# Chunk-selecting attention with a soft mixture of experts: selection masks of two score groups side by side in 32-row strips, and a new order of pair and slot steps

## The chip, the cores and the metric

The kernel runs on one core of a Trainium2 chip. The metric is the device time of one execution in microseconds (us); lower is better. A core has a matrix engine (PE, which writes only to the accumulator memory PSUM), a vector engine (DVE), an activation engine (ACT), a general engine (POOL, which here masks tiles and issues most DMAs) and a DMA-issuing engine (SP). Each engine works through its own list of instructions in order; semaphores tie the lists together.

## The reference

`q`, `k`, `v` have shape (4 batches, 8 heads, 768 positions, 64). For every query an upper bound of its score with each of 24 chunks of 32 keys decides which 6 chunks it may look at; then comes ordinary causal attention over these chunks. The result, seen as a 3072 x 512 matrix, goes through a soft mixture of 8 experts with 4 slots each.

```python
k_min = np.min(k_chunks, axis=3); k_max = np.max(k_chunks, axis=3)
ub = np.sum(np.maximum(q * k_min, q * k_max), axis=-1)        # per query and chunk
ub = np.where(causal, ub, -1e9)
top_chunks = np.argsort(ub, axis=-1)[..., -6:]
scores = scale * (q @ k.T), where (key's chunk in top_chunks) and (key <= query), else -1e9
attn = softmax(scores) @ v
x = attn as (3072, 512)
logits = x @ phi                                               # 32 slots
slot_input = softmax(logits over all 3072 rows).T @ x
slot_out = per expert: relu(slot_input @ w1) @ w2
out = softmax(logits over slots) @ slot_out
```

## The kernel before

Work goes by pairs of heads: 16 pairs, 4 to a batch, the two heads of a pair in the upper and lower 64 partitions. `qT` and `kT` hold a pair's queries and keys transposed (64 + 64 partitions x 768).

**Pair steps.** `transposes` and `evac_T` make `kT` and `qT` (PE into the PSUM tile `tr_ps`, then one ACT copy each). `kmin`, `kmax`, `qsplit` (DVE) and `ubound` (PE) give the chunk bounds in `ub_ps`; `ubound` starts each of its six query tiles with a matmul of its own that adds the causal bound (L229), followed by two matmuls (L234). `select` (twelve MAX8 and one compare on DVE, one small cast on POOL) writes to `ns_t`, for each query, a 1 at every chunk that is not selected, and the row's largest bound. `ns_transposes` and `evac_ns` turn it round into `nsT`, so that a matmul with the fixed matrix `smask` can add a large negative number to the scores of chunks that are left out.

**Scores.** The causal half of a pair's score matrix is cut into six groups, `GROUPS` 0 to 5, of widths 512, 512, 512, 512 (in two pieces of 256), 512 (384 and 128) and 128 per head. `scores(i, g)` issues for each piece a K.Q matmul for each head (L274) and then a mask matmul for each head (L280). Both kinds work on 64 rows, the two heads on different rows. A group's PSUM tile `sc_ps` has one bank for each head. `expo(i, g)` is one ACT exponential over the whole group (L292), followed by POOL's causal select of the diagonal blocks (L294). `pv` multiplies with V (L311), `normalise` divides (L324), `x_transposes` and `evac_x` store the pair's output transposed.

**Slot steps**, once per batch: `moe_logits`, `moe_copy`, `moe_max`, `moe_bound` (the maximum of the logits over rows), `moe_exp` (broadcast by PE, subtraction on DVE, exponential on ACT, rescaling of the running sum `si_acc`), `moe_comb` (exponentials over slots into `c_pad`), `moe_dispatch` (slot inputs, 30 matmuls into `si_ps`) and `moe_ct` (transposes of `c_pad`).

**Buffers.** PSUM is full: `p_sc` has two `sc_ps` tiles, `p_at` one tile for `pv`, and `p_tp` two buffers that all other PSUM tiles (`ub_ps`, `tr_ps` of keys and of queries, `xT_ps`, `ns_ps`, `pmT_ps`, `bc_ps`, `si_ps`, `cT_ps`, `lg_ps`) take in turn in the order of issue. So the first write to such a tile waits until the tile two before it in this order has been read out.

**Order.** It is written out by hand in one loop, and no scheduler changes it (`tc.manual_schedule()`). Iteration `i` handles the scores of pair `i`, the bounds of pair `i + 1`, the transposes of pair `i + 2`, `pv` of pair `i - 1` and the normalisation of pair `i - 2`; slot steps of a batch are put in at `i - 2` and `i - 3` past its last pair. In outline:

```python
scores/expo 0, scores/expo 1, [moe_max], ubound, normalise, [moe_bound], select,
transposes k + ACT copy, loads, pv 0-2, [moe_exp], scores/expo 2, scores/expo 3,
x_transposes, pv 3, transposes q + ACT copy, kmin, evac_x, kmax, [moe_comb], loads,
scores/expo 4, scores/expo 5, ns_transposes + evac_ns, pv 4, [moe_dispatch], pv 5,
qsplit, [moe_ct], [moe_logits, moe_copy]
```

After the loop come the last pairs' normalisation, the last batch's slot steps, the experts and the output.

Of the kernel before, what the change touches and what calls it, by code (L numbers as in the profile page):

```python
# [10 lines left out]
F32 = mybir.dt.float32  # L11
BF16 = mybir.dt.bfloat16
ALU = mybir.AluOpType
ACT = mybir.ActivationFunctionType
# [4 lines left out]
CH = 32  # L19
NCHUNK = 24  # L20
NQT = 6
P = 128
# [24 lines left out]
def kernel(  # L47
# [10 lines left out]
    nc = tc.nc  # L58
# [18 lines left out]
    st = {}  # L77
# [23 lines left out]
    smask = static.tile([P, NQT, 4, CH], BF16, name="smask")  # L101
    schunk = static.tile([P, NCHUNK, 1], BF16, name="schunk")
    headsel = static.tile([P, 1, 2, 1], BF16, name="headsel")
    ns_t = [static.tile([P, NQT, 2, 64], BF16, name=f"ns_t{i}") for i in range(2)]

    small = ctx.enter_context(tc.tile_pool(name="small", bufs=1))
    xp = ctx.enter_context(tc.tile_pool(name="xp", bufs=2))
# [50 lines left out]
        out=caus[:4], in_=caus[:4], compare_op=ALU.is_ge, fill=NEG, base=0,  # L158
        pattern=[[4, NQT], [0, 2], [-1, NCHUNK]], channel_multiplier=1,
    )  # L160
    for h in range(2):
        sl = schunk[h * 64:(h + 1) * 64]
        nc.gpsimd.affine_select(
            out=sl, in_=sl, compare_op=ALU.not_equal, fill=NEG, base=0,
            pattern=[[-1, NCHUNK], [0, 1]], channel_multiplier=1,
        )
        nc.gpsimd.affine_select(
            out=sl, in_=sl, compare_op=ALU.not_equal, fill=-1.0, base=-NCHUNK,
            pattern=[[0, NCHUNK], [0, 1]], channel_multiplier=1,
        )  # L170
# [54 lines left out]
    def ubound(i):  # L225
        ps = p_tp.tile([P, NQT, 2 * NCHUNK], F32, name="ub_ps", tag="tp")
        qpn, bd = st.pop(("qpn", i)), st.pop(("bd", i))
        for t in range(NQT):
            nc.tensor.matmul(  # L229
                ps[:, t, :], lhsT=qgrp.rearrange("p a b -> p (a b)"),  # L230
                rhs=caus[:, t].rearrange("p h c -> p (h c)"), start=True, stop=False,
            )
            for x in range(2):
                nc.tensor.matmul(  # L234
                    ps[:, t, :], lhsT=qpn[:, x, t * P:(t + 1) * P],
                    rhs=bd[:, x].rearrange("p h c -> p (h c)"),
                    start=False, stop=(x == 1),
                )
        st["ubps", i] = ps

# [12 lines left out]
    def ns_transposes(i):  # L253
        ps = p_tp.tile([P, NQT, P], BF16, name="ns_ps", tag="tp")
        for t in range(NQT):
            nc.tensor.matmul(  # L256
                ps[:, t, :], lhsT=ns_t[i % 2][:, t].rearrange("p h c -> p (h c)"),
                rhs=ident, is_transpose=True,
            )
        st["nsps", i] = ps  # L260

    def evac_ns(i):
# [1 line left out]
        nc.vector.tensor_copy(t, st.pop(("nsps", i)).rearrange("p t c -> p (t c)"))  # L264
        st["nsT", i] = t

    def scores(i, g):
        ps = p_sc.tile([P, 2, 512], F32, name="sc_ps", tag="sc")
        kT, qT, nsT = st["kT", i], st["qT", i], st["nsT", i]
        for kg, q0, w, c in GROUPS[g]:  # L270
            qs = slice(kg * P + q0, kg * P + q0 + w)
            for h in range(2):
                r = slice(h * 64, (h + 1) * 64)
                nc.tensor.matmul(  # L274
                    ps[:, h, c:c + w], lhsT=kT[r, kg * P:(kg + 1) * P], rhs=qT[r, qs],
                    start=True, stop=False,
                )
            for h in range(2):
                r = slice(h * 64, (h + 1) * 64)
                nc.tensor.matmul(  # L280
                    ps[:, h, c:c + w], lhsT=smask[r, kg].rearrange("p a b -> p (a b)"),
                    rhs=nsT[r, qs], start=False, stop=True,
                )
        st["scps", i, g] = ps

    def expo(i, g):
        w = WIDTH[g]
        if g < 5:
            e = ep.tile([P, 2, 512], BF16, name="e_sb", tag="e_sb")
        else:  # L290
            e = ep5.tile([P, 2, P], BF16, name="e5_sb", tag="e5_sb")
        nc.scalar.activation(e[:, :, :w], st.pop(("scps", i, g))[:, :, :w], func=ACT.Exp, scale=scale)  # L292

        nc.gpsimd.affine_select(  # L294
            out=e[:, :, :P], in_=e[:, :, :P], compare_op=ALU.is_ge, fill=0.0,
            base=0, pattern=[[0, 2], [1, P]], channel_multiplier=-1,
        )
        st["e", i, g] = e
# [81 lines left out]
        nc.vector.tensor_reduce(mb, pmT, axis=AX.X, op=ALU.max)  # L380
        st["mb", b] = mb

    def moe_exp(b):
        lg = st["lg", b]
        bc = p_tp.tile([P, NS], F32, name="bc_ps", tag="tp")
        nc.tensor.matmul(
            bc, lhsT=st.pop(("mb", b)).broadcast_to([NS, P]), rhs=identf[:NS, :NS], start=True, stop=True,
        )
        m_new, m_old = m_run[b % 2], m_run[(b + 1) % 2]
        if b == 0:  # L390
            nc.vector.tensor_copy(m_new, bc)
        else:
            nc.vector.tensor_tensor(m_new, m_old, bc, op=ALU.max)
        ld = small.tile([P, NQT, NS], F32, name="ld", tag="ld")
        nc.vector.tensor_tensor(
            ld, lg, m_new.rearrange("p (o s) -> p o s", o=1).broadcast_to([P, NQT, NS]), op=ALU.subtract,
        )
        d_sb = small.tile([P, NQT, NS], BF16, name="d_sb", tag="d_sb")
        nc.scalar.activation(d_sb, ld, func=ACT.Exp)
        st["d", b] = d_sb  # L400
        if b > 0:

            dm = small.tile([P, 1, NS], F32, name="dm", tag="dm")
            nc.vector.tensor_tensor(dm[:, 0, :], m_old, m_new, op=ALU.subtract)
            nc.scalar.activation(dm, dm, func=ACT.Exp)
            if b == B - 1:
                moe_comb(b)
            nc.vector.tensor_tensor(si_acc, si_acc, dm.broadcast_to([P, NDG + 1, NS]), op=ALU.mult)

    def moe_comb(b):  # L410

        lg = st.pop(("lg", b))
        rm = small.tile([P, NQT, 1], F32, name="rm", tag="rm")
        nc.vector.tensor_reduce(rm, lg, axis=AX.X, op=ALU.max)
        lc = small.tile([P, NQT, NS], F32, name="lc", tag="lc")
        nc.vector.tensor_tensor(lc, lg, rm.broadcast_to([P, NQT, NS]), op=ALU.subtract)

        for g in range(2):
            nc.scalar.activation(
                c_pad[:, :, :, g * SPE:(g + 1) * SPE],  # L420
                lc[:, :, g * 16:(g + 1) * 16].rearrange("p t (j s) -> p t j s", j=4), func=ACT.Exp,
            )
# [27 lines left out]
    def have(i):  # L450
        return 0 <= i < NPAIR

    def moe(step, i):

        if have(i) and i % NPB == NPB - 1:
            step(i // NPB)
# [15 lines left out]
    for i in range(-2, NPAIR):  # L472
        if i >= EARLY:
            wt = ctx.enter_context(tc.tile_pool(name=f"wt{i}", bufs=1))
            w_sb.append(wt.tile([P, NFG * Dm], BF16, name=f"w_sb{i}"))
            weights(i)
        if have(i):
            scores(i, 0)
            expo(i, 0)
            scores(i, 1)  # L480
            expo(i, 1)
        moe(moe_max, i - 3)
        if have(i + 1):
            ubound(i + 1)
        if have(i - 2):
            normalise(i - 2)
        moe(moe_bound, i - 3)
        if have(i + 1):
            select(i + 1)
        if have(i + 2):  # L490
            transposes(i + 2, "k")
            evac_T(i + 2, "k")
        if have(i + 4) and i >= -1:
            load(i + 4, "k")
            load(i + 4, "q")
        if have(i - 1):
            pv(i - 1, [0, 1, 2])
        moe(moe_exp, i - 3)
        if have(i):
            scores(i, 2)  # L500
            expo(i, 2)
            scores(i, 3)
            expo(i, 3)
        if have(i - 2):
            x_transposes(i - 2)
        if have(i - 1):
            pv(i - 1, [3])
        if have(i + 2):
            transposes(i + 2, "q")
            evac_T(i + 2, "q")  # L510
            kmin(i + 2)
        if have(i - 2):
            evac_x(i - 2)
        if have(i + 2):
            kmax(i + 2)
        moe(moe_comb, i - 3)
        if have(i + 2) and i >= 0:
            load_v(i + 2)
        if i < EARLY:
            weights(i)  # L520
        if have(i):
            scores(i, 4)
            expo(i, 4)
            scores(i, 5)
            expo(i, 5)
        if have(i + 1):
            ns_transposes(i + 1)
            evac_ns(i + 1)
        if have(i - 1):
            pv(i - 1, [4])  # L530
        moe(moe_dispatch, i - 3)
        if have(i - 1):
            pv(i - 1, [5])
        if have(i + 2):
            qsplit(i + 2)
        moe(moe_ct, i - 3)
        moe(moe_logits, i - 2)
        moe(moe_copy, i - 2)
        if i == LAST - 2:
            l_ctx.close()  # L540
        if i == LAST - 1:
            u_ctx.close()
# [21 lines left out]
    moe_copy(B - 1)  # L564
    moe_max(B - 1)
    moe_bound(B - 1)
    moe_exp(B - 1)
    moe_dispatch(B - 1)


# [88 lines left out]
    n = 0  # L659
# [46 lines left out]
```

## Time and profile before

| | us |
|---|---|
| median of 3 runs | 177.5 (176.98 to 177.66) |
| the profiled execution | 178.38 |
| its span in the trace | 176.7 |
| PE busy in the span | 139.9 (79%) |
| DVE busy | 127.9 (72%) |
| ACT busy | 119.8 (68%) |
| POOL busy | 99.8 (57%) |

The profiled execution took 1.7 us more than the span that the trace shows, and 0.9 us more than the median. Three views are used. The page sums up each engine and the costliest groups of instructions. The windows view gives each engine's busy time within a stretch. The timeline lists instructions in order of time: start, length, engine, line, what is written and read, how many of them were merged, and in brackets the idle time ahead with what ended it. Matmuls overlap, so that the distance from one start to the next, and not the length, tells how long PE is taken. The head loop runs from the first exponential at 16.94 us to about 137 us.

### The profile page before, as it was taken

Reading aid. Unit: us, or ns where it says so; the run is one execution under the profiler, and the core shown is the slowest. Engines: PE = TensorE matmul, PEld = TensorE weight load, DVE = VectorE, ACT = ScalarE, POOL = GpSimd, SP = SyncE. Lnnn points to the kernel's source line nnn. Section 1 sums busy time; section 2 is a strip of 40 time slices with the busy share of each in tenths; the row PEclk is TensorE's granted clock in tenths of the full one; section 3 lists DMA queues with packets and bytes.
Section 4 is the critical chain, followed back from the end, with each engine's and each line's share of the span. In section 5 each row is a group of like instructions: output and inputs, shape, how many; then the busy total and the mean of one; then the engine's idle time right before and its main releaser. Section 6 shows DMA issues by size and latency. Waiting matters only on the chain.

```text
span 176.7 us, 5992 instructions
## 1 busy us (share of the span) xinstructions
PE 139.9 (79%) x2485; PEld 96.1 (54%) x2486; DVE 127.9 (72%) x429; ACT 119.8 (68%) x163; POOL 99.8 (57%) x194
## 2 busy tenths in 40 slices
PE   0447989999989889999988999999689569976400
PEld 0333656667667667766766776676467443532000
DVE  4177759999999998999998999999752650247530
ACT  2414799889889868988977698898668321156430
POOL 8975677887779657878774676659344600000000
PEclk9999999999999999999999999999999956999855
DMA  3999999999999999999999999299999994009995
GB/s 41 152 183 165 208 209 200 205 201 201 183 214 189 210 183 123 208 174 206 164 139 201 170 198 149 22 182 210 194 213 218 211 217 81 4 6 403 401 406 211
DMA packets 40459, 32.92 MB, mean 186 GB/s; under 512 B 26352, under 2 KB 34544, under 8 KB 40432
## 3 DMA queue, kind: packets, MB, share of 16 engines
q0 software_dynamic: 38416, 26.25, 101.2%
q1 hardware_dynamic: 2016, 6.29, 9.0%
q8 instruction: 19, 0.31, 0.7%
q14 instruction: 8, 0.07, 0.1%
HBM read 52.49 MB, written 6.29 MB: 333 GB/s over the span
## 4 chain that ended last, share of the span: by engine, by line
PE 37%; ACT 22%; POOL 11%; DVE 11%; DMA 10%; issue 6%; POOLq 0%; DVEq 0%; ACTq 0%
ACT e_sb L292 17%; PE sc_ps L274 7%; DMA out_dram<-o_sb 5%; PE at_ps L311 5%; PE sc_ps L280 5%; DMA k_in<-in_k_dram 4%; POOL e_sb L294 4%; PE tr_ps L187 3%; PE h_ps L603 3%; DVE x_sb L324 3%; POOL q_in L132 2%; PE so_ps L638 2%; POOL k_in L132 2%; PE si_ps L430 2%; PE ns_ps L256 2%
## 5 line engine op out<-in xcount | busy, mean ns | idle before, releaser
L292 ACT ACTIVATE e_sb<-sc_ps 128x1024 bf16<-128x1024 f32 x96 | 83.6, 935 | 11.8 <-PE sc_ps L280 10.9
L294 POOL TENSOR_SCALAR_AFFINE_SELECT e_sb<-e_sb 128x256 bf16<-128x256 bf16 x96 | 39.4, 421 | 32.9 <-ACT e_sb L292 32.1
L274 PE MATMUL sc_ps<-qT,kT 64*128 64x512 bf16 (+3 forms) x256 | 40.3, 315 | 5.7 <-ACT e_sb L292 5.4
L280 PE MATMUL sc_ps<-nsT,smask 64*128 64x512 bf16 (+3 forms) x256 | 37.4, 311 | 0.5 <-DVE nsT L264 0.5
L311 PE MATMUL at_ps<-v_t,e_sb 128*128 128x65 bf16 x672 | 29.4, 194 | 1.2 <-DVE x_sb L324 1.1
L311 PEld LDWEIGHTS <-e_sb 128*128 128x128 bf16 x672 | 25.1, 98 | 3.4 <-DVE x_sb L324 1.6
L274 PEld LDWEIGHTS <-kT 64*128 64x128 bf16 x256 | 15.7, 95 | 16.0 <-issue 8.2
L245 DVE MAX8 mx<-ub_ps 128x8 f32<-128x24 f32 x192 | 18.8, 172 | 5.7 <-PE ub_ps L234 5.6
L205 DVE TENSOR_REDUCE mm<-kT 128x24 bf16<-128x768 bf16 x16 | 15.2, 950 | 5.8 <-ACT kT L196 5.8
L137 POOL DMA_DIRECT2D v_t<-in_v_dram x16 | 16.7, 1042 | 2.0 <-PE ns_ps L256 1.3
L196 ACT COPY kT<-tr_ps 128x768 bf16<-128x768 bf16 x16 | 12.8, 803 | 5.4 <-PE tr_ps L187 5.4
L280 PEld LDWEIGHTS <-smask 64*128 64x128 bf16 x256 | 13.3, 96 | 5.6 <-issue 1.5
L324 DVE TENSOR_TENSOR x_sb<-at_ps,inv 128x768 bf16<-128x768 f32 (+2 forms) x17 | 15.5, 911 | 0.6
L211 DVE TENSOR_REDUCE mm<-kT 128x24 bf16<-128x768 bf16 x16 | 15.1, 943 | 0.0
L187 PE MATMUL tr_ps<-ident,k_in 128*64 128x128 bf16 x192 | 9.4, 240 | 6.4 <-DMA k_in<-in_k_dram 5.3
L196 ACT COPY qT<-tr_ps 128x768 bf16<-128x768 bf16 x16 | 13.2, 825 | 0.9 <-PE tr_ps L187 0.9
L668 DVE TENSOR_SCALAR o_sb<-o_ps,cinv 128x512 f32<-128x512 f32 x12 | 8.6, 747 | 7.1 <-PE o_ps L666 4.5
L132 POOL DMA_DIRECT2D k_in<-in_k_dram x16 | 11.7, 728 | 0.9 <-issue 0.5
L234 PE MATMUL ub_ps<-bd,qpn 128*128 128x48 bf16 x192 | 10.2, 187 | 2.3 <-DVE qpn L221 2.2
L670 ACT ACTIVATE o_sb<-o_ps,cinv 128x512 f32<-128x512 f32 x12 | 7.8, 688 | 5.7 <-DMA out_dram<-o_sb 3.3
L229 PEld LDWEIGHTS <-qgrp 128*128 128x128 bf16 x96 | 8.0, 98 | 6.7 <-issue 6.7
L132 POOL DMA_DIRECT2D q_in<-in_q_dram x16 | 11.5, 716 | 0.0
(95 smaller groups left out, 213.3 us busy)
## 6 DMA issues: line engine op xcount, KB each, us to landing
w_sb<-in_moe_w_dram POOLq DMA_DIRECT2D x16, 1024.0 KB, 11.5
out_dram<-o_sb SPq DMA_DIRECT2D x10, 512.0 KB, 5.5
k_in<-in_k_dram POOLq DMA_DIRECT2D x16, 192.0 KB, 7.3
q_in<-in_q_dram POOLq DMA_DIRECT2D x16, 192.0 KB, 7.9
v_t<-in_v_dram POOLq DMA_DIRECT2D x16, 192.0 KB, 7.6
out_dram<-o_sb SPq DMA_DIRECT2D x4, 256.0 KB, 3.4
phi_sb<-in_moe_phi_dram POOLq DMA_DIRECT2D x1, 32.0 KB, 8.7
```

The lines of the kernel that those rows point to most:

```text
L132: nc.gpsimd.dma_start(out=t, in_=src.rearrange("h (p g) d -> p h (g d)", p=P))
L137: nc.gpsimd.dma_start(out=v_t[i % NV][:, :, :, :D], in_=v[b, 2 * j:2 * j + 2].rearrange("h (g p) d -> p h g d", p=P),)
L196: nc.scalar.copy(t.rearrange("d (p g) -> d p g", g=NQT), st.pop((nm + "ps", i)).rearrange("d g p -> d p g"),)
L205: nc.vector.tensor_reduce(mm[:, 0, 0, :], kT, axis=AX.X, op=ALU.min)
L211: nc.vector.tensor_reduce(mm[:, 1, 0, :], kT, axis=AX.X, op=ALU.max)
L245: nc.vector.max(mx[:, a, :], ub[:, a, :])
L274: nc.tensor.matmul(ps[:, h, c:c + w], lhsT=kT[r, kg * P:(kg + 1) * P], rhs=qT[r, qs], start=True, stop=False,)
L280: nc.tensor.matmul(ps[:, h, c:c + w], lhsT=smask[r, kg].rearrange("p a b -> p (a b)"), rhs=nsT[r, qs], start=False, stop=True,)
L292: nc.scalar.activation(e[:, :, :w], st.pop(("scps", i, g))[:, :, :w], func=ACT.Exp, scale=scale)
L294: nc.gpsimd.affine_select(out=e[:, :, :P], in_=e[:, :, :P], compare_op=ALU.is_ge, fill=0.0, base=0, pattern=[[0, 2], [1, P]], channel_mult ...
L311: nc.tensor.matmul(o, lhsT=st["e", i, g][:, h, c:c + P], rhs=v_t[i % NV][:, h, kg, :], start=(kg == 0), stop=(kg == t),)
L324: nc.vector.tensor_tensor(st["x", b][:, t0:t1, 2 * j:2 * j + 2, :].rearrange("p t h d -> p h t d"), at[:, :, :, :D], inv.broadcast_to([P, ...
```

## The change

- `ns_t` has 32 columns for each head in place of 64, and `ns_transposes` transposes it twice for each query tile, into partitions 0 to 63 and 64 to 127 (12 matmuls in place of 6): the mask operand then stands in four strips of 32 partitions, two copies of two heads. `schunk`, from which `smask` is made, is filled for four strips in place of two.
- `scores(i, g0)` handles two groups at once: the K.Q matmuls of both groups, each of 64 rows as before, and then the mask matmuls of both, each of 32 rows in a strip of its own. `expo` of the two groups follows.
- `ubound` adds the causal bound with one matmul of 288 columns in place of six of 48.
- `moe_exp` is split into `moe_shift` (PE and DVE), `moe_exp` (the two exponentials) and `moe_rescale`; `moe_comb` into `moe_comb` (DVE) and `moe_weights` (ACT).
- The order: `pv` 4 and `ns_transposes` with `evac_ns` stand ahead of groups 4 and 5; `moe_max` and `moe_bound` stand there too, behind them; `moe_shift` and `moe_comb` stand at the end of the iteration; `moe_exp`, `moe_rescale`, `moe_weights`, `moe_dispatch` and `moe_ct` come one iteration later than before.

```diff
@@ -101,7 +101,7 @@
     smask = static.tile([P, NQT, 4, CH], BF16, name="smask")
     schunk = static.tile([P, NCHUNK, 1], BF16, name="schunk")
     headsel = static.tile([P, 1, 2, 1], BF16, name="headsel")
-    ns_t = [static.tile([P, NQT, 2, 64], BF16, name=f"ns_t{i}") for i in range(2)]
+    ns_t = [static.tile([P, NQT, 2, CH], BF16, name=f"ns_t{i}") for i in range(2)]
 
     small = ctx.enter_context(tc.tile_pool(name="small", bufs=1))
     xp = ctx.enter_context(tc.tile_pool(name="xp", bufs=2))
@@ -158,8 +158,8 @@
         out=caus[:4], in_=caus[:4], compare_op=ALU.is_ge, fill=NEG, base=0,
         pattern=[[4, NQT], [0, 2], [-1, NCHUNK]], channel_multiplier=1,
     )
-    for h in range(2):
-        sl = schunk[h * 64:(h + 1) * 64]
+    for r in range(4):
+        sl = schunk[r * CH:(r + 1) * CH]
         nc.gpsimd.affine_select(
             out=sl, in_=sl, compare_op=ALU.not_equal, fill=NEG, base=0,
             pattern=[[-1, NCHUNK], [0, 1]], channel_multiplier=1,
@@ -225,16 +225,16 @@
     def ubound(i):
         ps = p_tp.tile([P, NQT, 2 * NCHUNK], F32, name="ub_ps", tag="tp")
         qpn, bd = st.pop(("qpn", i)), st.pop(("bd", i))
+        nc.tensor.matmul(
+            ps.rearrange("p t c -> p (t c)"), lhsT=qgrp.rearrange("p a b -> p (a b)"),
+            rhs=caus.rearrange("p t h c -> p (t h c)"), start=True, stop=False,
+        )
         for t in range(NQT):
-            nc.tensor.matmul(
-                ps[:, t, :], lhsT=qgrp.rearrange("p a b -> p (a b)"),
-                rhs=caus[:, t].rearrange("p h c -> p (h c)"), start=True, stop=False,
-            )
             for x in range(2):
                 nc.tensor.matmul(
                     ps[:, t, :], lhsT=qpn[:, x, t * P:(t + 1) * P],
                     rhs=bd[:, x].rearrange("p h c -> p (h c)"),
-                    start=False, stop=(x == 1),
+                    start=False, stop=(t == NQT - 1 and x == 1),
                 )
         st["ubps", i] = ps
 
@@ -253,10 +253,11 @@
     def ns_transposes(i):
         ps = p_tp.tile([P, NQT, P], BF16, name="ns_ps", tag="tp")
         for t in range(NQT):
-            nc.tensor.matmul(
-                ps[:, t, :], lhsT=ns_t[i % 2][:, t].rearrange("p h c -> p (h c)"),
-                rhs=ident, is_transpose=True,
-            )
+            for r in range(2):
+                nc.tensor.matmul(
+                    ps[r * 64:(r + 1) * 64, t, :], lhsT=ns_t[i % 2][:, t].rearrange("p h c -> p (h c)"),
+                    rhs=ident, is_transpose=True,
+                )
         st["nsps", i] = ps
 
     def evac_ns(i):
@@ -264,24 +265,32 @@
         nc.vector.tensor_copy(t, st.pop(("nsps", i)).rearrange("p t c -> p (t c)"))
         st["nsT", i] = t
 
-    def scores(i, g):
-        ps = p_sc.tile([P, 2, 512], F32, name="sc_ps", tag="sc")
+    def scores(i, g0):
         kT, qT, nsT = st["kT", i], st["qT", i], st["nsT", i]
-        for kg, q0, w, c in GROUPS[g]:
-            qs = slice(kg * P + q0, kg * P + q0 + w)
-            for h in range(2):
-                r = slice(h * 64, (h + 1) * 64)
-                nc.tensor.matmul(
-                    ps[:, h, c:c + w], lhsT=kT[r, kg * P:(kg + 1) * P], rhs=qT[r, qs],
-                    start=True, stop=False,
-                )
-            for h in range(2):
-                r = slice(h * 64, (h + 1) * 64)
-                nc.tensor.matmul(
-                    ps[:, h, c:c + w], lhsT=smask[r, kg].rearrange("p a b -> p (a b)"),
-                    rhs=nsT[r, qs], start=False, stop=True,
-                )
-        st["scps", i, g] = ps
+        tiles = [p_sc.tile([P, 2, 512], F32, name="sc_ps", tag="sc") for _ in range(2)]
+        for n, ps in enumerate(tiles):
+            for m, (kg, q0, w, c) in enumerate(GROUPS[g0 + n]):
+                qs = slice(kg * P + q0, kg * P + q0 + w)
+                for h in range(2):
+                    r = slice(h * 64, (h + 1) * 64)
+                    nc.tensor.matmul(
+                        ps[:, h, c:c + w], lhsT=kT[r, kg * P:(kg + 1) * P], rhs=qT[r, qs],
+                        start=(m == 0), stop=False,
+                    )
+            st["scps", i, g0 + n] = ps
+        for m in range(2):
+            for n, ps in enumerate(tiles):
+                pieces = GROUPS[g0 + n]
+                if m >= len(pieces):
+                    continue
+                kg, q0, w, c = pieces[m]
+                qs = slice(kg * P + q0, kg * P + q0 + w)
+                for h in range(2):
+                    r = slice((2 * n + h) * CH, (2 * n + h + 1) * CH)
+                    nc.tensor.matmul(
+                        ps[:, h, c:c + w], lhsT=smask[r, kg].rearrange("p a b -> p (a b)"),
+                        rhs=nsT[r, qs], start=False, stop=(m == len(pieces) - 1),
+                    )
 
     def expo(i, g):
         w = WIDTH[g]
@@ -380,7 +389,7 @@
         nc.vector.tensor_reduce(mb, pmT, axis=AX.X, op=ALU.max)
         st["mb", b] = mb
 
-    def moe_exp(b):
+    def moe_shift(b):
         lg = st["lg", b]
         bc = p_tp.tile([P, NS], F32, name="bc_ps", tag="tp")
         nc.tensor.matmul(
@@ -395,16 +404,24 @@
         nc.vector.tensor_tensor(
             ld, lg, m_new.rearrange("p (o s) -> p o s", o=1).broadcast_to([P, NQT, NS]), op=ALU.subtract,
         )
+        st["ld", b] = ld
+        if b > 0:
+
+            dm = small.tile([P, 1, NS], F32, name="dm", tag="dm")
+            nc.vector.tensor_tensor(dm[:, 0, :], m_old, m_new, op=ALU.subtract)
+            st["dm", b] = dm
+
+    def moe_exp(b):
         d_sb = small.tile([P, NQT, NS], BF16, name="d_sb", tag="d_sb")
-        nc.scalar.activation(d_sb, ld, func=ACT.Exp)
+        nc.scalar.activation(d_sb, st.pop(("ld", b)), func=ACT.Exp)
         st["d", b] = d_sb
         if b > 0:
-
-            dm = small.tile([P, 1, NS], F32, name="dm", tag="dm")
-            nc.vector.tensor_tensor(dm[:, 0, :], m_old, m_new, op=ALU.subtract)
+            dm = st["dm", b]
             nc.scalar.activation(dm, dm, func=ACT.Exp)
-            if b == B - 1:
-                moe_comb(b)
+
+    def moe_rescale(b):
+        if b > 0:
+            dm = st.pop(("dm", b))
             nc.vector.tensor_tensor(si_acc, si_acc, dm.broadcast_to([P, NDG + 1, NS]), op=ALU.mult)
 
     def moe_comb(b):
@@ -414,7 +431,11 @@
         nc.vector.tensor_reduce(rm, lg, axis=AX.X, op=ALU.max)
         lc = small.tile([P, NQT, NS], F32, name="lc", tag="lc")
         nc.vector.tensor_tensor(lc, lg, rm.broadcast_to([P, NQT, NS]), op=ALU.subtract)
-
+        st["lc", b] = lc
+
+    def moe_weights(b):
+
+        lc = st.pop(("lc", b))
         for g in range(2):
             nc.scalar.activation(
                 c_pad[:, :, :, g * SPE:(g + 1) * SPE],
@@ -477,14 +498,12 @@
         if have(i):
             scores(i, 0)
             expo(i, 0)
-            scores(i, 1)
             expo(i, 1)
-        moe(moe_max, i - 3)
+        moe(moe_exp, i - 4)
         if have(i + 1):
             ubound(i + 1)
         if have(i - 2):
             normalise(i - 2)
-        moe(moe_bound, i - 3)
         if have(i + 1):
             select(i + 1)
         if have(i + 2):
@@ -495,12 +514,12 @@
             load(i + 4, "q")
         if have(i - 1):
             pv(i - 1, [0, 1, 2])
-        moe(moe_exp, i - 3)
         if have(i):
             scores(i, 2)
             expo(i, 2)
-            scores(i, 3)
             expo(i, 3)
+        moe(moe_rescale, i - 4)
+        moe(moe_weights, i - 4)
         if have(i - 2):
             x_transposes(i - 2)
         if have(i - 1):
@@ -513,7 +532,15 @@
             evac_x(i - 2)
         if have(i + 2):
             kmax(i + 2)
-        moe(moe_comb, i - 3)
+        if have(i - 1):
+            pv(i - 1, [4])
+        if have(i + 1):
+            ns_transposes(i + 1)
+            evac_ns(i + 1)
+        moe(moe_max, i - 3)
+        moe(moe_bound, i - 3)
+        moe(moe_dispatch, i - 4)
+        moe(moe_ct, i - 4)
         if have(i + 2) and i >= 0:
             load_v(i + 2)
         if i < EARLY:
@@ -521,19 +548,13 @@
         if have(i):
             scores(i, 4)
             expo(i, 4)
-            scores(i, 5)
             expo(i, 5)
-        if have(i + 1):
-            ns_transposes(i + 1)
-            evac_ns(i + 1)
-        if have(i - 1):
-            pv(i - 1, [4])
-        moe(moe_dispatch, i - 3)
         if have(i - 1):
             pv(i - 1, [5])
         if have(i + 2):
             qsplit(i + 2)
-        moe(moe_ct, i - 3)
+        moe(moe_shift, i - 3)
+        moe(moe_comb, i - 3)
         moe(moe_logits, i - 2)
         moe(moe_copy, i - 2)
         if i == LAST - 2:
@@ -564,7 +585,11 @@
     moe_copy(B - 1)
     moe_max(B - 1)
     moe_bound(B - 1)
+    moe_shift(B - 1)
     moe_exp(B - 1)
+    moe_comb(B - 1)
+    moe_weights(B - 1)
+    moe_rescale(B - 1)
     moe_dispatch(B - 1)
```

More of the change, by code (lines that the diff above doesn't have):

```diff
@@ L397, in moe_exp @@
         )
-        d_sb = small.tile([P, NQT, NS], BF16, name="d_sb", tag="d_sb")
-        nc.scalar.activation(d_sb, ld, func=ACT.Exp)
-        st["d", b] = d_sb
+        st["ld", b] = ld
         if b > 0:
@@ L404, in moe_exp @@
             nc.vector.tensor_tensor(dm[:, 0, :], m_old, m_new, op=ALU.subtract)
+            st["dm", b] = dm
+    def moe_exp(b):
+        d_sb = small.tile([P, NQT, NS], BF16, name="d_sb", tag="d_sb")
+        nc.scalar.activation(d_sb, st.pop(("ld", b)), func=ACT.Exp)
+        st["d", b] = d_sb
+        if b > 0:
+            dm = st["dm", b]
             nc.scalar.activation(dm, dm, func=ACT.Exp)
-            if b == B - 1:
-                moe_comb(b)
+    def moe_rescale(b):
+        if b > 0:
+            dm = st.pop(("dm", b))
             nc.vector.tensor_tensor(si_acc, si_acc, dm.broadcast_to([P, NDG + 1, NS]), op=ALU.mult)
```

## The prediction

> **What bounds the kernel now.** I read the page first, then a plain iteration of the loop against one with slot steps, then the timeline of the plain one.
>
> ```profile
> PE 139.9 (79%) x2485; PEld 96.1 (54%) x2486; DVE 127.9 (72%) x429; ACT 119.8 (68%) x163; POOL 99.8 (57%) x194
> L292 ACT ACTIVATE e_sb<-sc_ps 128x1024 bf16<-128x1024 f32 x96 | 83.6, 935 | 11.8 <-PE sc_ps L280 10.9
> ```
> ```profile
> core 0: us, PE busy (x) PEld busy (x) DVE busy (x) ACT busy (x) POOL busy (x), PEclk, DMA share, GB/s
> 60.03:69.54 9.51, 8.29 (x171) 6.22 (x167) 8.58 (x31) 7.26 (x11) 5.84 (x11) 1.00 1.26 160
> ...
> 76.39:83.24 6.85, 6.63 (x132) 4.85 (x128) 6.45 (x23) 6.37 (x8) 5.57 (x12) 1.00 1.39 196
> ```
>
> Each stretch runs from one pair's first exponential to the next pair's. In the plain iteration of 6.85 us PE, DVE and ACT all work 6.4 us or more: nobody has half a microsecond to spare, and what counts is how they hand work over. The timeline shows that, first PE's rows and then ACT's:
>
> ```profile
> 75.69 0.39 PE L274 MATMUL sc_ps<-qT,kT 64*128 64x512 bf16 x2 [0.19 <-ACT e_sb L292]
> 75.91 0.39 PE L280 MATMUL sc_ps<-nsT,smask 64*128 64x512 bf16 x2
> 76.12 0.39 PE L274 MATMUL sc_ps<-qT,kT 64*128 64x512 bf16 x2
> ...
> 78.82 0.27 PE L274 MATMUL sc_ps<-qT,kT 64*128 64x256 bf16 x2
> 78.93 0.27 PE L280 MATMUL sc_ps<-nsT,smask 64*128 64x256 bf16 x2
> 79.14 0.51 PE L333 MATMUL xT_ps<-ident,x_sb 128*128 128x128 bf16 x6
> ...
> 80.92 0.23 PE L274 MATMUL sc_ps<-qT,kT 64*128 64x128 bf16 x2
> ```
> ```profile
> 76.39 1.94 ACT L292 ACTIVATE e_sb<-sc_ps 128x1024 bf16<-128x1024 f32 x2 [0.48 <-PE sc_ps L280]
> 78.22 0.81 ACT L196 COPY kT<-tr_ps 128x768 bf16<-128x768 bf16 x1
> 78.90 1.97 ACT L292 ACTIVATE e_sb<-sc_ps 128x1024 bf16<-128x1024 f32 x2
> 80.72 0.84 ACT L196 COPY qT<-tr_ps 128x768 bf16<-128x768 bf16 x1
> 81.40 1.37 ACT L292 ACTIVATE e_sb<-sc_ps 128x1024 bf16<-128x1024 f32 x2
> 83.24 1.02 ACT L292 ACTIVATE e_sb<-sc_ps 128x1024 bf16<-128x1024 f32 x1 [0.48 <-PE sc_ps L280]
> ```
>
> ACT never pauses except ahead of group 0 (0.48 us). Two score buffers make that possible: while ACT reads one group, PE fills the next. Four prices stand in these rows. The two heads' 64-row matmuls run side by side: a pair of 512 columns takes PE 0.21 us (75.69, 75.91, 76.12), one of 256 takes 0.11. A matmul's end lies 0.39 us after its start (512 columns), 0.23 (128). ACT starts 0.09 after a mask has ended (75.91 + 0.39 to 76.39), PE 0.05 after ACT frees a buffer (78.90 + 1.97 = 80.87 to 80.92). And going from 64-row to 128-row matmuls costs about 0.10: 78.93 to 79.14 is 0.21 where 256 columns need 0.11.
>
> **Part 1: masks by fours.** PE saves the second pair of masks in each couple of groups, 0.21 + 0.21 + 0.05 us an iteration, and some 0.1 in the bounds (18 matmuls at 0.025 become one of 288 columns and 12); six more transposes and the switches of row mode take that back. It matters little, because the order puts a new wait in. Masks of both groups stand behind both K.Q products, and the second K.Q product needs the buffer that ACT's last exponential is still reading. So no score work of a couple can end while ACT works on the couple before: double buffering is gone, and after each second exponential ACT waits for this chain:
>
> 0.05 (buffer free) + 0.21 (K.Q of the second group) + 0.10 (switch to 32 rows) + 0.39 (masks) + 0.09 = 0.84 us.
>
> - Ahead of groups 0 and 1 no ACT work lies in it; before, the wait was 0.48. **+0.36.**
> - Ahead of groups 2 and 3 the kT copy covers part: ACT is back at exponentials 0.57 after the last one's end (76.39 + 1.94 = 78.33 to 78.90). 0.84 - 0.57 = **+0.27.**
> - Ahead of 4 and 5: `pv` 4 and the twelve transposes now precede them, so PE comes to group 5's K.Q about 0.05 late. 0.05 + 0.05 + 0.05 (128 columns) + 0.10 + 0.16 (384 columns) + 0.22 (the second mask piece) + 0.09 = 0.72, of which the qT copy covers 0.53 (80.87 to 81.40). **+0.19.**
>
> Together +0.82 us an iteration, 6.85 becoming 7.67. Other engines have room then: DVE's 6.45 and PE's work fit in 7.67, and the new place of `evac_ns` behind kmax still ends over 1 us ahead of the next masks.
>
> Two prices are not in the trace. It has no step from 64 to 32 rows: from below it costs nothing (L274 to L280, both of 64 rows, 0.21 for 512 columns), from above 0.10 (64 to 128, and 128 to 64 likewise). I take 0.10, since every change of shape that the trace shows paid it. At nothing, an iteration is 0.29 cheaper. The Trainium skill, "TensorEngine Tiling (Array Packing)", Key Properties, says that changing the tiling mode drains the engine; that would be the 0.10, and it speaks against this change, which adds three changes of mode an iteration.
>
> Four strips at once are not in the trace either: between 0.21 us for four 512-column masks (as free as two are) and 0.43 (two after two). I take 0.21, because the second head costs nothing in any row. At 0.43 the first group's masks still come first, so only PE gets late, ahead of groups 4 and 5: some +0.15 an iteration. The Trainium skill, "TensorE: Matmul & The Clock Gate", Part 3, gives 3.07 for the speedup of four 32-row tiles at 512 columns; by that the four take 4 x 0.21 / 3.07 = 0.28, an estimate, with 0.07 more for PE and +0.05 or so in an iteration's sum.
>
> Over iterations 0 to 13: 14 x 0.82 = 11.5. In iterations 0, 2 and 4 ACT already idles at the second place (by 1.26, 0.27 and 0.27 beyond the plain one) and hides some: -0.5. **+11.0.**
>
> **Part 2: slot steps.** Before, they lengthen iterations 5, 6, 9, 10, 13 and 14 by 0.34, 2.66, 0.34, 3.61, 0.33 and 2.36 us over 6.85. ACT's view of iteration 6 says why:
>
> ```profile
> 62.24 0.80 ACT L196 COPY kT<-tr_ps 128x768 bf16<-128x768 bf16 x1 [0.27 <-PE tr_ps L187]
> 64.15 0.36 ACT L399 ACTIVATE d_sb<-ld 128x192 bf16<-128x192 f32 x1 [1.11 <-DVE ld L395]
> ...
> 67.35 0.46 ACT L419 ACTIVATE c_pad<-lc 128x96 bf16<-128x96 f32 x2 [0.32 <-DVE lc L416]
> ```
>
> ACT stands at slot exponentials whose inputs DVE has not made yet. One iteration later the inputs are long there, and these waits go. The logits (24 x 0.025 us) go into PE's new idle time at no cost; without it they cost the 0.34 again. But `moe_max`, `moe_dispatch` and `moe_ct` now stand ahead of groups 4 and 5, and the `p_tp` order makes `pmT_ps` and `si_ps` wait for the buffer two before, the queries' `tr_ps`, which ACT's qT copy frees 0.69 us after the fourth exponential's end (80.87 to 81.56). PE runs in order, so groups 4 and 5 wait behind them.
>
> - First iteration: 0.69 + 0.05 + 0.20 (pmT) + 0.27 (K.Q of both groups) + 0.10 + 0.16 + 0.22 + 0.09 = 1.78 after that exponential, against 0.72: **+1.06.**
> - Second: the slot exponentials put 0.46 on ACT ahead of the kT copy (0.27 of it in the new wait: +0.19) and `c_pad` 0.36 ahead of the qT copy. Then 0.69 + 0.36 + 0.05 + 0.75 (30 matmuls at 0.025) + 0.34 (six transposes) + 0.10 + 0.27 + 0.10 + 0.16 + 0.22 + 0.09 = 3.13, against 0.72: +2.41, in all **+2.60.**
>
> Batches 0 and 1 pay 2 x 3.66 = 7.3; before, iterations 5, 6, 9, 10 and 13 paid 7.28. **0.** Batch 2 leaves iteration 14, which has no kT and qT copies and takes 7.62 in place of 9.21: **-1.6**; in iteration 15 exponential 4 must wait for `c_pad`, its transposes and the couple's chain, about 6.4 us after exponential 0 and not 4.16: +2.2, of which the tail's DVE work hides about 0.3: **+1.9.** The tail keeps its order and cost.
>
> **Sum:** 178.4 + 11.0 + 0 - 1.6 + 1.9 = 189.7 for a profiled execution; the median lies 0.9 below, so 188.8 us.
>
> **Rivals.**
> - *The switch to 32 rows is free* (20%): 15 x 0.29 = 4.4 less, 184.4. For it: masks and K.Q read the same partitions. Against it: every change of shape in the trace paid. Were the slot waits gone as well (the next but one case), it would be about 178, no change.
> - *Strips go two after two, or slot steps wait longer than worked out* (15%): 15 x 0.15 = 2.3 to 5 more, 191 to 194. So the masks would not run as the change says.
> - *Faster* (5%): the slot waits decide. Should pmT and dispatch not wait for the qT copy, a batch would pay some 0.4 us (its ACT work, less what falls in idle time), the loop would gain 7.3 - 0.8 + 1.6 - 1.9 = 6.2 us, and the couples would have to stay under 6.2 / 15 = 0.41 us an iteration. With a free switch they cost 0.53; with the chain wholly covered at two of the three places and 0.26 at the first, 3.9, the time would be 177.5 - 6.2 + 3.9 = 175. For it: ACT's idle time above. Against it: `tr_ps` and the buffer order leave no choice.
> - My own sum: 60%, 186 to 191.5.
>
> About 0.5% is what a measurement can tell from no change here: slower by more than that has 92%, within it 3% (out of the free switch's 20%), faster 5%. The range, 182.5 to 194, takes in both bounds of the two unknown prices and 2 us either way for the slot steps.
>
> **What would show it.** The changed profile should have ACT's plain period near 7.67; idle time of ACT ahead of exponentials 0, 2 and 4, put down to PE's mask line, of 0.84, 0.27 and 0.19 us; the couples' second K.Q released by ACT; mask starts in fours 0.21 apart or less; pmT and `si_ps` released by ACT's qT copy; PE's busy time down. A plain period near 6.85 would prove me wrong at the double buffering, one near 7.4 at the switch, and slot iterations of under 8 us at the buffer order.

## The result, and the profile after

The changed kernel takes 192.36 us (median of 4 runs, 190.67 to 193.35) against 177.58 us: 1.082 times the time before, with a 95% interval of 1.076 to 1.088. A second set of runs beside the experiments gave 1.079 (1.073 to 1.085). The profiled execution took 191.45 us, its span is 189.7 us. From here on a time in us that is said to be above the kernel before is the measured ratio less 1, times 177.5; runs over 1.5% slower than the fastest of the same kernel are left out of ratios.

From the pages, the mask matmul before (L280), and then of the changed kernel the engines' totals, the exponential (now L301) and the mask matmul (now L290):

```profile
L280 PE MATMUL sc_ps<-nsT,smask 64*128 64x512 bf16 (+3 forms) x256 | 37.4, 311 | 0.5 <-DVE nsT L264 0.5
```
```profile
PE 142.5 (75%) x2502; PEld 92.0 (48%) x2502; DVE 130.4 (69%) x429; ACT 121.6 (64%) x163; POOL 100.0 (53%) x198
...
L301 ACT ACTIVATE e_sb<-sc_ps 128x1024 bf16<-128x1024 f32 x96 | 82.8, 915 | 29.3 <-PE sc_ps L290 28.3
...
L290 PE MATMUL sc_ps<-nsT,smask 32*128 32x512 bf16 (+3 forms) x256 | 19.6, 319 | 0.1
```

The masks' busy time fell from 37.4 to 19.6 us, as the change set out to do. (Matmuls of different lines overlap, so a line's busy time is not what it costs: that of K.Q, whose matmuls are the same, fell from 40.3 to 31.2, and PE's as a whole rose from 139.9 to 142.5.) But ACT's idle time ahead of exponentials rose from 11.8 to 29.3 us, nearly all of it put down to those masks. That rise is not a price by itself: idle time that stood ahead of copies and slot exponentials has moved there too, and e3 below, only 1.8 us slower than the kernel before, has 20.4 us of it. The period is what counts. Iteration 9 shows where it grows; it holds a batch's logits as well, and iteration 8, which has no slot steps, has the same period (timeline of the changed kernel, ACT):

```profile
93.10 1.94 ACT L301 ACTIVATE e_sb<-sc_ps 128x1024 bf16<-128x1024 f32 x2 [0.87 <-PE sc_ps L290]
94.92 0.81 ACT L196 COPY kT<-tr_ps 128x768 bf16<-128x768 bf16 x1
95.91 1.94 ACT L301 ACTIVATE e_sb<-sc_ps 128x1024 bf16<-128x1024 f32 x2 [0.18 <-PE sc_ps L290]
97.73 0.81 ACT L196 COPY qT<-tr_ps 128x768 bf16<-128x768 bf16 x1
98.67 1.30 ACT L301 ACTIVATE e_sb<-sc_ps 128x1024 bf16<-128x1024 f32 x2
100.83 1.02 ACT L301 ACTIVATE e_sb<-sc_ps 128x1024 bf16<-128x1024 f32 x1 [0.86 <-PE sc_ps L290]
```

The period is 100.83 - 93.10 = 7.73 us in place of 6.85. ACT waits 0.87 ahead of group 0, 0.18 more after the kT copy, and 0.13 after the qT copy (97.73 + 0.81 to 98.67). PE's rows of the same stretch give the reason:

```profile
94.40 0.39 PE L276 MATMUL sc_ps<-qT,kT 64*128 64x512 bf16 x2
95.09 0.39 PE L276 MATMUL sc_ps<-qT,kT 64*128 64x256 bf16 x4 [0.30 <-ACT e_sb L301]
95.42 0.40 PE L290 MATMUL sc_ps<-nsT,smask 32*128 32x512 bf16 x6
95.78 0.49 PE L342 MATMUL xT_ps<-ident,x_sb 128*128 128x128 bf16 x6
...
99.74 0.67 PE L276 MATMUL sc_ps<-qT,kT 64*128 64x512 bf16 x4
100.34 0.40 PE L290 MATMUL sc_ps<-nsT,smask 32*128 32x512 bf16 x4
100.67 0.30 PE L228 MATMUL ub_ps<-caus,qgrp 128*128 128x288 bf16 x1
```

K.Q of group 2 (94.40) is done early. K.Q of group 3 (95.09) waits until ACT has finished with group 1 (93.10 + 1.94 = 95.04), and only behind it come the masks of both groups, at 95.42. From group 3's K.Q to the masks PE needs 0.33 where its columns fill 0.21; four 512-column masks start together at 100.34, and the next step follows 0.33 later where 0.21 would do. So strips do go four at a time for about the price of one, and each change of row mode costs some 0.11; how far the trace can tell the two apart is said with the prediction's steps below.

### The profile page after: what moved, and what is told of

Read it like the earlier page. It is cut to its first block, busy times and chain, and to the rows that moved or that the text cites. A ratio compares the mean times of both kernels' runs of the same rounds, so it can differ in the third digit from the quotient of the medians.

```text
span 189.7 us, 6039 instructions
## 1 busy us (share of the span) xinstructions
PE 142.5 (75%) x2502; PEld 92.0 (48%) x2502; DVE 130.4 (69%) x429; ACT 121.6 (64%) x163; POOL 100.0 (53%) x198
## 4 chain that ended last, share of the span: by engine, by line
PE 44%; ACT 27%; DMA 8%; DVE 7%; issue 6%; POOL 4%; SPq 0%; ACTq 0%; POOLq 0%; DVEq 0%
ACT e_sb L301 21%; PE sc_ps L276 10%; PE sc_ps L290 7%; PE tr_ps L187 5%; PE at_ps L320 4%; DMA out_dram<-o_sb 4%; DMA k_in<-in_k_dram 4%; PE h_ps L628 3%; ACT qT L196 3%; PE ub_ps L234 2%; PE so_ps L663 2%; PE xT_ps L342 2%; DVE x_sb L333 2%; PE ub_ps L228 1%; PE si_ps L451 1%
## 5 line engine op out<-in xcount | busy, mean ns | idle before, releaser
L301 ACT ACTIVATE e_sb<-sc_ps 128x1024 bf16<-128x1024 f32 x96 | 82.8, 915 | 29.3 <-PE sc_ps L290 28.3
L303 POOL TENSOR_SCALAR_AFFINE_SELECT e_sb<-e_sb 128x256 bf16<-128x256 bf16 x96 | 38.9, 413 | 49.2 <-ACT e_sb L301 49.0
L276 PE MATMUL sc_ps<-qT,kT 64*128 64x512 bf16 (+3 forms) x256 | 31.2, 315 | 11.7 <-ACT e_sb L301 11.2
L320 PE MATMUL at_ps<-v_t,e_sb 128*128 128x65 bf16 x672 | 31.9, 196 | 3.2 <-DVE x_sb L333 2.4
L276 PEld LDWEIGHTS <-kT 64*128 64x128 bf16 x256 | 11.8, 94 | 22.8 <-issue 17.8
L290 PE MATMUL sc_ps<-nsT,smask 32*128 32x512 bf16 (+3 forms) x256 | 19.6, 319 | 0.1
L132 POOL DMA_DIRECT2D k_in<-in_k_dram x16 | 11.6, 728 | 0.7 <-issue 0.5
L125 POOL DMA_DIRECT2D w_sb<-in_moe_w_dram x16 | 11.4, 715 | 0.0
L691 PE MATMUL o_ps<-so_sb,cT_all 128*128 128x512 bf16 x24 | 7.6, 405 | 4.7 <-DVE o_sb L693 3.7
L187 PE MATMUL tr_ps<-ident,q_in 128*64 128x128 bf16 x192 | 9.1, 234 | 2.0 <-DMA q_in<-in_q_dram 1.1
```

What stands on the lines that cost most here:

```text
L132: nc.gpsimd.dma_start(out=t, in_=src.rearrange("h (p g) d -> p h (g d)", p=P))
L187: nc.tensor.matmul(ps[h * 64:(h + 1) * 64, g, :], lhsT=src[:, h, g * D:(g + 1) * D], rhs=ident, is_transpose=True,)
L276: nc.tensor.matmul(ps[:, h, c:c + w], lhsT=kT[r, kg * P:(kg + 1) * P], rhs=qT[r, qs], start=(m == 0), stop=False,)
L290: nc.tensor.matmul(ps[:, h, c:c + w], lhsT=smask[r, kg].rearrange("p a b -> p (a b)"), rhs=nsT[r, qs], start=False, stop=(m == len(pieces) ...
L303: nc.gpsimd.affine_select(out=e[:, :, :P], in_=e[:, :, :P], compare_op=ALU.is_ge, fill=0.0, base=0, pattern=[[0, 2], [1, P]], channel_mult ...
L320: nc.tensor.matmul(o, lhsT=st["e", i, g][:, h, c:c + P], rhs=v_t[i % NV][:, h, kg, :], start=(kg == 0), stop=(kg == t),)
```

## The experiments

**e1: the couples alone.** On the kernel before: four strips, K.Q of two groups and then their masks, everything else as it was.

```diff
-    expo(i, 0); scores(i, 1); expo(i, 1)        # likewise 2, 3 and 4, 5
+    expo(i, 0); expo(i, 1)                      # scores(i, 0) handles both
```

> The kernel before, with the couples alone: four strips, 12 transposes, K.Q of two groups and then their masks in fours; causal bound, slot steps and all other order as before. Theory (double buffering lost): the three waits of a couple come back whatever the slot steps do, so the plain period goes from 6.85 to about 7.7 us and the start is 1.4 us later: 15 x 0.85 + 1.4 = 14 us, about 191.5 us. Rival (the new order of slot steps and of pv 4 is what costs): near the time before, 178 to 180 us. Second rival (clock): the time is that of the theory, and granted clock under 0.95.

Measured: 193.27 us, 1.086 (1.078 to 1.095), or 15.3 us above. The plain period is 7.62 us. So the couples, strips included, bring the whole loss without any new order of slot steps. Granted clock was 0.946 to 0.962 in these runs, so that a lower clock is not needed for it.

**e2: couples with masks of 64 rows.** The changed kernel, its order kept, but two strips and six transposes, so no change of mode between K.Q and masks.

```diff
-                    r = slice((2 * n + h) * CH, (2 * n + h + 1) * CH)
+                    r = slice(h * 64, (h + 1) * 64)
```

> The changed kernel, but with masks of 64 rows as before (two strips, 6 transposes), still in the order of couples: K.Q, K.Q, masks, masks. It has no change of row mode and no strips. Theory: the wait stays, shorter by the switch of 0.10 at each of three places and by 0.1 or so ahead of groups 4 and 5: plain period 7.35 to 7.45, start 1.4 earlier, so 192.4 - 4.5 - 1.4 = about 186.5 us. Rival (the 32-row strips and their switch are the whole cost): 178 to 180 us.

Measured: 185.56 us, 1.042 (1.030 to 1.055), 7.5 us above. Its plain iteration, ACT:

```profile
88.73 1.94 ACT L300 ACTIVATE e_sb<-sc_ps 128x1024 bf16<-128x1024 f32 x2 [0.76 <-PE sc_ps L289]
...
96.27 1.02 ACT L300 ACTIVATE e_sb<-sc_ps 128x1024 bf16<-128x1024 f32 x1 [0.76 <-PE sc_ps L289]
```

The wait ahead of group 0 stays at 0.76; the switch was 0.11 of 0.87. The period is 7.54, against 7.35 to 7.45 expected: ahead of groups 4 and 5 the switch turned out to be no part of the wait (PE comes late there), so only two places gained.

**e3: the new order alone.** The changed kernel with scores and masks of the kernel before, group by group.

```diff
-    scores(i, 0); expo(i, 0); expo(i, 1)                # couples
+    scores(i, 0); expo(i, 0); scores(i, 1); expo(i, 1)  # likewise 2, 3 and 4, 5
```

> The changed kernel with scores and masks as before (64 rows, each group with its own masks, group by group), so that double buffering is back; the new order of slot steps, pv 4 and transposes stays. Theory: groups 0 to 3 no longer wait; pv 4 and ns_transposes ahead of groups 4 and 5 make PE some 0.2 us late there, and pmT, dispatch and ct still wait there for the qT copy: about 7 us over three batches, as before the change. Plain period 6.85 to 7.1, about 178 to 181 us. Rival (the order is the larger part of the loss): 186 us or more.

Measured: 1.010 (1.006 to 1.014), 1.8 us above, median 179.46. ACT's plain iteration:

```profile
84.59 1.94 ACT L292 ACTIVATE e_sb<-sc_ps 128x1024 bf16<-128x1024 f32 x2 [0.48 <-PE sc_ps L280]
86.42 0.81 ACT L196 COPY kT<-tr_ps 128x768 bf16<-128x768 bf16 x1
87.09 1.97 ACT L292 ACTIVATE e_sb<-sc_ps 128x1024 bf16<-128x1024 f32 x2
88.91 0.85 ACT L196 COPY qT<-tr_ps 128x768 bf16<-128x768 bf16 x1
89.92 1.30 ACT L292 ACTIVATE e_sb<-sc_ps 128x1024 bf16<-128x1024 f32 x2 [0.16 <-PE sc_ps L280]
```

The wait at group 0 is 0.48 again, and the wait at group 2 is gone. e2 and e3 differ in nothing but the order of K.Q and masks within a couple: 64-row masks in both, the same bounds, slot steps and copies. That order alone turns 7.11 us an iteration into 7.54, and 1.010 into 1.042. This is the lost double buffering, shown by itself. What remains is the wait ahead of group 4 (0.16, the period 7.11 and not 6.85). I put it down to the new place of `pv` 4 and the transposes: in e6, where they stand as before the change, that wait is gone and iteration 3 takes 6.85 again.

**e4: slot steps behind the scores.** The changed kernel with `moe_max`, `moe_bound`, `moe_dispatch` and `moe_ct` behind `pv` 5.

```diff
-        moe(moe_max, i - 3); moe(moe_bound, i - 3); moe(moe_dispatch, i - 4); moe(moe_ct, i - 4)
         ...scores and exponentials 4, 5; pv 5
+        moe(moe_max, i - 3); moe(moe_bound, i - 3); moe(moe_dispatch, i - 4); moe(moe_ct, i - 4)
```

> The changed kernel with moe_max, moe_bound, moe_dispatch and moe_ct moved behind groups 4 and 5 and pv 5, so that nothing of the scores waits behind the tiles that wait for the qT copy. Theory: the first slot iteration loses its 1.0 us, the second keeps 0.5 to 1 us of its 2.4: 7.5 us become 2 to 3, so about 187.5 us, with a plain period of 7.73 unchanged. Rival (slot steps cost by their PE work, wherever it stands): 191 to 192.5 us.

Measured: 189.58 us, 1.065 (1.056 to 1.075), 11.6 us above and some 3 below the changed kernel; I had expected 5. In the loop the theory held: iterations 6, 7, 10 and 11 took 0.07, 0.81, 0.07 and 1.28 us over the plain period, 2.2 together, where the changed kernel's took 7.55. The end lost some of it: from iteration 15's first exponential to the end the profile has 48.6 us in place of 46.95. Two things stand there. Batch 2's dispatch and transposes, 1.1 us of PE (145.15 to 146.23), come between the last scores and the last pair's `pv`; and in this profile the granted clock was at half from 137.87 to 144.70 us, over all of pair 15's scores, where the changed kernel's was at full. In e9, the changed kernel again, half clock from 144.23 to 147.64 us, at the same place, cost nothing by the end (46.9), which speaks for the dispatch; no run separates the two.

**e5: the start.** The changed kernel with ACT's copy that makes `smask` behind pair 0's kT and qT copies, and pair 2's loads ahead of the first weight, V and phi loads.

```diff
-    nc.scalar.copy(smask, schunk broadcast)     # ahead of the loop
+    load(2, "k"); load(2, "q")                  # ahead of load_w(0)
     ...evac_T(i + 2, "q")
+    if i == -2: nc.scalar.copy(smask, schunk broadcast)
```

> The changed kernel with its start alone altered: ACT's copy that makes smask comes after the first two pairs of copies' first pair (behind kT and qT of pair 0) in place of ahead of them, and the loads of pair 2 are issued ahead of the first weight, V and phi loads. Theory: the four more fills of schunk on POOL (0.4 us each) cost 1.4 us only because ACT waits for them with its smask copy, ahead of the kT copy; so the first exponential comes at 16 us or earlier in place of 18.3, and the time falls by 1.5 to 3 us, to 189.5 to 191. Rival (the start is set by the loads): first exponential not before 18 us and the time as it was.

Measured: 188.61 us, 1.059 (1.052 to 1.067), 4 us below the changed kernel's ratio. ACT at the start, first the kernel before, then the changed kernel and then e5:

```profile
6.83 0.83 ACT L171 COPY smask<-schunk 128x768 bf16<-128x768 bf16 x1 [4.06 <-POOL schunk L167]
```
```profile
8.41 0.83 ACT L171 COPY smask<-schunk 128x768 bf16<-128x768 bf16 x1 [5.64 <-POOL schunk L167]
9.15 0.79 ACT L196 COPY kT<-tr_ps 128x768 bf16<-128x768 bf16 x1
...
18.31 1.02 ACT L301 ACTIVATE e_sb<-sc_ps 128x1024 bf16<-128x1024 f32 x1 [1.56 <-PE sc_ps L290]
```
```profile
5.89 0.80 ACT L195 COPY kT<-tr_ps 128x768 bf16<-128x768 bf16 x1 [3.81 <-PE tr_ps L186]
...
16.56 1.02 ACT L300 ACTIVATE e_sb<-sc_ps 128x1024 bf16<-128x1024 f32 x1 [3.03 <-PE sc_ps L289]
```

With four strips POOL fills `schunk` in eight steps and not four; ACT stood at the `smask` copy until 8.41 us (6.83 before the change) with the kT copy queued behind it. The first exponential moved from 16.94 to 18.31 us, and in e5 back to 16.56. That the strips set this start can be seen in the other runs too: e2, e3 and e6, with two strips, begin at 16.7, and e4, e8 and e9, with four, at 18.3.

The gain is larger than expected, and the second half of the edit, the earlier loads, has a part in it. Iterations 0 and 1 took 7.46 and 7.56 us in e5, and 8.16 each in the changed kernel's profile. The same kernel run again (e9) had no half-clock window there (see the last section), as e5 had none: its iteration 1 took 7.56 too, but its iteration 0 took 9.08. There PE waits for pair 2's keys:

```profile
20.29 0.85 PE L187 MATMUL tr_ps<-ident,k_in 128*64 128x128 bf16 x12 [1.17 <-DMA k_in<-in_k_dram]
```

The changed kernel's profile has the same wait, of 1.02 us, and e5's has none. So beyond the start, iteration 0 gained by the loads. The clock can account for iteration 1, and for iteration 6 (8.75 us in place of 9.34).

**e6: only the split slot steps.** Scores, masks, `pv` 4 and transposes as before the change, the slot steps as in e4, the bounds with one causal matmul.

```diff
+        moe(moe_exp, i - 4)                             # behind exponential 1
+        moe(moe_rescale, i - 4); moe(moe_weights, i - 4) # behind exponential 3
+        moe_max, moe_bound, moe_dispatch, moe_ct, moe_shift, moe_comb   # behind pv 5
```

> A version that tries to beat both: scores, masks (64 rows), pv 4 and ns_transposes as before the change, from the change only the split slot steps (exponentials one iteration later) and the one causal matmul, with moe_max, moe_bound, moe_dispatch and moe_ct behind pv 5. Theory: plain period 6.85 as before; the 9.6 us that slot steps added to six iterations fall to 4 to 6 us (their PE work, 0.6, 0.5 and 1.1 us a batch, comes on top of a full PE, and 0.8 us on ACT), so 173 to 175 us. Rival (the slot steps' cost is work, and not waits): 176.5 to 178.

Measured: 1.004 (1.000 to 1.009), about 178.2 us: no gain; the rival was the nearer one, with 178 as its upper end. ACT no longer waits for slot inputs, but over iterations 5 to 13 the slot steps still add 6.9 us (7.28 before). In its profile PE waits 5.2 us, 8 times, at `pv` for DVE's normalisation, which stands behind the slot steps' DVE work; before, it was 1.1 us, twice. DVE was as full as ACT, so I read this as one wait gone and the work behind it come up; no run takes the new wait away to prove it.

**e7: e6 with e5's start.**

```diff
+    load(2, "k"); load(2, "q")                  # ahead of load_w(0)
+    if i == -2: nc.scalar.copy(smask, schunk broadcast)
```

> The kernel of the run before with the altered start (smask copy behind the first kT and qT copies, pair 2's loads first). Theory: the first exponential comes 1.5 to 3 us earlier than 16.9 and the time falls by 1 to 3 us against that run: 171 to 173.5. Rival (loads set the start): no difference between the two.

Measured: 177.79 us, 1.000 (0.995 to 1.004). The first exponential came at 15.04 us, 1.7 earlier than in e6, but the ratio fell only by 0.005, about 0.8 us, a little under the 1 to 3 expected; and with e6's miss in it the time is far from 171 to 173.5. No version here beats the kernel before.

**e8 and e9: is it the clock?** e8 issues the twelve transposes of `ns_transposes` four times over in six iterations; e9 is the changed kernel again.

```diff
-        for t in range(NQT):
+        for t in list(range(NQT)) * times:      # 4 in iterations 0, 1, 6, 7, 10, 11
```

> The changed kernel with more PE work: in iterations 0, 1, 6, 7, 10 and 11 the twelve transposes of ns_transposes are issued four times over (36 more, about 1.0 us), writing the same values. In 6, 7, 10 and 11 they stand where PE waits for the qT copy 0.9 to 1.1 us anyway. Theory (clock: a part of the loss, and the spread between runs, comes from 3.4 us windows of half clock that follow stretches in which PE idles): no half-clock window in iterations 0 to 11, granted clock 0.95 or more in most runs, and 1 to 2 us less than the changed kernel beside it, although it does more. Rival (the windows cost nothing on this path): the same time, or up to 2 us more for iterations 0 and 1.

> The changed kernel as it is, on the same chip beside the run before. Both theories: 190.5 to 193.5 us; theory of the clock: runs with a granted clock near 0.93 lie about 2 us above runs near 0.954.

Measured: e8 1.090 (1.082 to 1.097), e9 1.079 (1.073 to 1.085). e8's profile has no half-clock window before pair 15's scores, but neither has e9's, and the added work was not free: exponential 4 comes 0.21 us later in iterations 6 and 10 and 0.9 and 0.7 in 7 and 11. In e9 the run at clock 0.937 took 192.69 and one at 0.955 took 192.34, so the clock does not order the runs. My theory on the spread fell; what sets it stays open.

## Why the prediction was right, and where it was short

The forecast was 188.8 us (182.5 to 194.0); 192.36 lies in the range. By its steps:

- *Double buffering is lost at three places:* right, and shown by e2 against e3. Period 7.73 (forecast 7.67). The distances between exponentials give +0.31, +0.30 and +0.26 for the three places, forecast +0.36, +0.27 and +0.19. The third was put too low: PE comes to group 4's K.Q at 97.80, and 0.23 later to group 5's, which is 0.12 after the buffer is free (97.85 + 0.05) and not 0.05. The logits cost nothing, as forecast: iterations 5, 9 and 13 have the plain period.
- *The switch to 32 rows costs 0.10:* right (0.33 for 0.21 in PE's rows, 0.76 against 0.87 of wait in e2). The bound at nothing is out, and so is the rival built on it. The Trainium skill, "TensorEngine Tiling (Array Packing)", Key Properties, says that changing the tiling mode drains the engine. The 0.10 to 0.11 measured here agrees with that, but no run shows that it is a drain.
- *Four strips go at once:* right, as far as the trace can split the sum. The measured 0.33 from four 512-column masks to the next step holds the masks and a switch. Where groups 4 and 5 end with only two masks of 128 columns, the next step starts 0.15 later, in 15 of the 16 iterations, where the columns fill 0.05: a switch from 32 to 128 rows is 0.10. That leaves 0.23 for the four, against 0.21 for one width and 0.43 for two after two. The Trainium skill, "TensorE: Matmul & The Clock Gate", Part 3, gives 3.07 for the speedup of four 32-row tiles at 512 columns; the estimate from it, 4 x 0.21 / 3.07 = 0.27 (the prediction wrote 0.28), would leave only 0.06 for the switch, so this trace speaks against it here.
- *pmT and dispatch wait for the qT copy:* right. The changed kernel's rows on PE:

```profile
71.24 0.28 PE L382 MATMUL pmT_ps<-identf,pm 128*32 128x128 f32 x1 [0.73 <-ACT qT L196]
...
81.15 0.75 PE L451 MATMUL si_ps<-d_sb,x_sb 128*128 128x32 bf16 x24 [1.06 <-ACT qT L196]
```

  Iterations 6, 7, 10 and 11 took 1.60, 2.55, 1.01 and 2.40 us over the period, 7.55 together against 7.3 forecast. The closeness is in part luck: the first two hold a half-clock window, and in e9, without one, the four took 6.96.
- *Batch 2 leaves iteration 14:* 7.62 us forecast and measured. From iteration 15 on: +1.3, forecast +1.9. Exponential 4 came 6.49 us after exponential 0, as worked out (6.4); the term that was mis-sized is what the tail hides of these 2.3 us more, put at 0.3 and measured 1.1.
- *The start costs nothing* is the step that failed. The sum had no term for `schunk`'s four more fills, although the profile before shows ACT waiting 4.1 us for `schunk` (6.83 in e5's rows). It is 1.4 us, in front of everything. A change to a one-off preparation must be followed through the queue of each engine like a step of the loop.
- *PE's busy time goes down,* one of the signs, did not come: it rose from 139.9 to 142.5 us. Part of that is the clock (e5, at full clock in the loop, has 140.9), but in iteration 8, at full clock, it is 6.75 us where the kernel before has 6.63. Why is not shown: e2, which has neither strips nor these switches, has 142.3.
- Over the profiled execution the sum is therefore 12.0 (iterations 0 to 13, forecast 11.0) - 1.6 + 1.3 + 1.4 = 13.1 us, against 11.3. And the profiled run of the changed kernel lies 0.9 below its median, where that of the kernel before lay 0.9 above: this is another 1.8 us, with no cause that I could show.

By parts, going from the kernel before to the changed one: the new order 1.8 us (e3), K.Q of two groups ahead of masks 5.7 (e2 less e3), strips, switches and start 7.1 (the rest; of it the profiles of e2 and of the changed kernel show 5.6, 1.6 of it at the start, and the other 1.5 has no place that I could find). e1 shows that this isn't additive: with the couples and the old order the time is the same as with the new.

## What to carry to other kernels

Packing matmuls saves time on the matrix engine only if the tiles that they need at once leave the other buffers free: here four masks side by side need both score buffers, and the reader of these buffers was the engine with no time to spare. Before a merge of steps, follow each buffer: who frees it, and what of the merged step stands behind that wait. Where three engines are all near full, taking away one wait (e6) only shows the next engine's work.

## What I had not expected of the hardware

In the changed kernel's profile the granted clock falls to half within the loop, which the profile before does not show. It is no property of the kernel: the second profile of the same kernel (e9) stays at full clock until pair 15's scores. The clock row of the changed kernel's page, with PE's busy tenths:

```profile
PE   0347679889789989879899786989896758988320
...
PEclk9999969999999997999999999999999985999855
```

Slices 6 and 16 (4.74 us each, counted from 1) hold a half-clock window of 3.4 us, at 25.6 and 73.4 us; the windows before them had PE busy 1.55 and 2.38 of 3.41 us. The first covers the first 2.5 us of iteration 1, which took 8.16 us, and 7.56 at full clock in e9. The second fell into iteration 6: 9.34 us, while iteration 10, which does the same work at full clock, took 8.75; in e9 iteration 6 took 8.96. So a window went with some 0.4 to 0.6 us in the iteration where it fell. Other windows of that length with 2.3 to 2.5 us of work (at 18.8 and 80.2 us in this profile) were not followed by half clock, and e8 could not show that keeping PE busy pays, so what sets it off stays open.
